# Sums in front of half-size matrix products: twelve of them on GpSimd

## The chip, the cores and the metric

One Trainium2 chip, one of its cores. The metric is the time of one execution of the kernel on the device in microseconds (us). Runs of the kernel before: median 295.94 us, from 295.76 to 295.99. Engines are called as in the profile: PE (TensorE, matrix products), PEld (its weight loads), DVE (VectorE), ACT (ScalarE), POOL (GpSimd), SP (SyncE, here only a queue of DMA issues).

## The reference

Attention with a sliding window of 128 and a linear bias, for 8 batches x 8 heads x 576 positions x 64, and behind it a two-layer network with squared ReLU on the 4608 x 512 result:

```
rel = pos[:, None] - pos[None, :]
scores = scale * q @ k^T - slope_h * |rel|,  masked to 0 <= rel < 128
attn = softmax(scores);  x = (attn @ v) as 4608 x 512
h = x @ w_in              # 512 x 2048
g = relu(h) ** 2
out = g @ w_out           # 2048 x 512, float32
```

## The kernel before

The tokens are cut into 9 groups of 512 (`g` = 0 to 8). For each group the kernel makes the attention, then `h = x @ w_in` ("up"), then the squares, then `out = g @ w_out` ("down"). While the down products of group `g` run, the up products of group `g + 1` run between them, so that PE has always something to do. The last group has only its down products after it.

From group 1 on the down product is made with seven half-size products in place of eight (Strassen-Winograd): the 512 x 2048 block of squares `gs.tile` and `w_out` are each seen as 2 x 2 blocks, and sums of blocks are made in front. The four kinds of sums of the squares are `S1` to `S4` (function `prepare`, lines 1632 to 1662). Each is a bf16 tensor operation over 128 x 1024 elements, and each is cut into two halves `q` = 0, 1 by the feature blocks, so a group has eight of them:

- `S1` = A(21) + A(22), into `sums[:, 0]`; waits for the squares of the group's later 256 tokens (`c12`, `c22`).
- `S2` = S1 - A(11), into `sums[:, 1]`; waits for S1 and the squares of `c11`.
- `S3` = A(11) - A(21), in place in `gs.tile`; waits for S1, which reads the old values, and `c11`.
- `S4` = A(12) - S2, in place; waits for S2 and for product 2, which reads the old values.

Products are named `p<group>.<product>.<token half>`: eight matmuls of 128 x 128 by 128 x 256 (line 1516). Product 5 takes S1, product 6 takes S2, product 7 takes S3, product 3 takes S4; products 1, 2 and 4 take squares as they are. `sums` has one buffer for S1 and one for S2, so S1 of the next group waits until product 5 of this group is done, and S2 until product 6 is.

From group 6 on the up product is made with seven products too (function `up_product`, line 1353 issues its matmuls), for four slices `u` of the features: `f<group>.<u>.<product>`, four matmuls each. Out of PSUM their results go by copies (`s1`, `s2`, `s5`, line 719 on DVE or 721 on ACT) and sums (`c11`, `c22`, `c12`, line 1374 on DVE), each with an ACT ReLU (`relu...`, line 1215) and a square (`sq...`, line 1227 on DVE, 1225 on ACT) behind it. A product of a slice waits for the copy or sum in front of it in the same bank: `f.4` for `c22`, `f.7` for `s2`, `f.6` for `s1`, `f.5` for `c11`, `f.3` for `s5`. The operands of the up products of a group are made by four sums `ut<group>.0` to `.3` (line 1320 on DVE). The down products leave PSUM the same way, by copies `s1_<g>`, `s2_<g>`, `s5_<g>`, `s3_<g>` and sums `c11_<g>` (line 1574), `c22_<g>` (1583), `c12_<g>` (1586). Of the attention, the masks `m<block>` (lines 1022 and 1029), the reciprocals and the normalisation (1121, 1130) are on DVE; its last block is done at about 231 us.

The order on each engine is not written out by hand. Each piece of work is a `Task` with its engine (some with two to choose from), a booked duration, a key, its dependencies and the buffers that it takes and gives back. `Plan.order` lists them once, before the program is written: it goes forward in a booked time and gives each engine the task that can start first, by key among those that can start about as soon. A table `ADJ` shifts keys by name. The program is then written in the order of the booked starts, and each engine works its list strictly in that order. So a changed engine or booked duration of one task changes the order of others, and the choice between DVE and ACT for squares and copies. POOL issues the loads of q, k, v and the weights (lines 812, 815, 867, 872), and does no arithmetic but the `iota` of line 735.

Of the kernel before, what the change touches and what calls it, by code (L numbers as in the profile page):

```python
# [29 lines left out]
S_LEAD = 60  # L30
# [580 lines left out]
def kernel(  # L611
    ctx: ExitStack, tc: tile.TileContext, q, k, v, moe_w_in, moe_w_out, out
):
    nc = tc.nc
# [73 lines left out]
    plan = Plan({**psum_bufs, "rec": 4, "rt": RT, "g": 2, "osb": OSB, "cs": CS, "ut": 2, "s1": 1, "s2": 1, "v0": B, "kqT0": B, "stage": 2, **size})  # L688
# [19 lines left out]
    def dve(n, rate=1):  # L708
        return n / rate / 0.96 + 68.0
# [42 lines left out]
    for part in (1, 0):  # L752
        key = EARLY + 2 if part else -1e5 + 1100
        mkey = -1e5 + 1000 if part else key
        t_dist[part] = plan.add({"DVE": 600.0}, key, lambda part=part: build_dist(part), [t_ident],
                                name=f"dist{part}", later=0.0 if part else 18000.0)
# [13 lines left out]
    for r in range(2):  # L770
        for c in range(4):
            def build_slope(r=r, c=c):
# [5 lines left out]
                else:  # L778
                    nc.scalar.activation(o, dist[:, 1], AF.Copy, bias=0.0, scale=f)
            t_slope[r].append(plan.add({"ACT": act(128), "DVE": dve(128)}, EARLY + 3 + r, build_slope, [t_dist[1]],  # L780
                                       name=f"slope{r}.{c}"))
# [9 lines left out]
    for i in range(size["v"]):  # L791
        t_one["v", i] = plan.add({"DVE": 50.0}, -1e5 + 900 + i, lambda i=i: ones(tiles["v"][i:i + 1]),
                                 name=f"one1.{i}", later=20000.0)
# [99 lines left out]
    def warm_up():  # L893
        bank(s_warm, "wm")
        for _ in range(N_WARM):
            nc.tensor.matmul(s_warm.tile, warm[:, 0:128], warm, start=True, stop=True)
    plan.add({"PE": 430.0 * min(8, N_WARM) + 216.0 * max(0, N_WARM - 8)}, EARLY, warm_up, [t_wz], [s_warm], [s_warm],
             name="warm")
# [728 lines left out]
    def g_sq_at(g):  # L1627
        def sq(half, parts):
            return [x for t in (2 * half, 2 * half + 1) for p in parts for x in sq_of[g, t, p]]
        return sq  # L1630

    def prepare(g, key):

        sq = g_sq_at(g)
        gs = g_slots[g]
        tags = ("ox", "oy") if g % 2 else ("oy", "ox")
        if g >= G_A:
            tags = ("a", "a")
        st = {"slot": {"X": Slot(tags[0]), "Y2": Slot(tags[1]), "Y5": Slot(tags[1]),
                       "S1": Slot("s1"), "S2": Slot("s2")},  # L1640
              "S1": [], "S2": [], "S3": [], "S4": []}
        A, Bk = slice(0, 256), slice(256, 512)

        def add(name, q, out_of, a_of, b_of, op, deps, acq, rel):
            def run():
                nc.vector.tensor_tensor(out_of(), a_of(), b_of(), op=op)  # L1646
            st[name].append(plan.add({"DVE": dve(1024, 2)}, key - S_LEAD + {"S1": 0, "S2": 1, "S3": 2, "S4": 30}[name], run,
                                     deps, acq, rel, name=f"{name}.{g}.{q}"))
        s = st["slot"]
        for q in range(2):  # L1650
            c, d = slice(4 * q, 4 * q + 4), slice(8 + 4 * q, 12 + 4 * q)
            add("S1", q, lambda c=c: sums[:, 0, c], lambda c=c: gs.tile[:, c, Bk], lambda d=d: gs.tile[:, d, Bk], ALU.add,
                sq(1, (q, q + 2)), [] if q else [s["S1"]], [gs])
            add("S2", q, lambda c=c: sums[:, 1, c], lambda c=c: sums[:, 0, c], lambda c=c: gs.tile[:, c, A], ALU.subtract,
                [st["S1"][q]] + sq(0, (q,)), [] if q else [s["S2"]], [gs, s["S1"]])
            add("S3", q, lambda c=c: gs.tile[:, c, Bk], lambda c=c: gs.tile[:, c, A], lambda c=c: gs.tile[:, c, Bk],
                ALU.subtract, [st["S1"][q]] + sq(0, (q,)), [], [gs])
        for q in range(2):
            c, d = slice(4 * q, 4 * q + 4), slice(8 + 4 * q, 12 + 4 * q)
            add("S4", q, lambda d=d: gs.tile[:, d, A], lambda d=d: gs.tile[:, d, A], lambda c=c: sums[:, 1, c],  # L1660
                ALU.subtract, [st["S2"][q]] + sq(0, (q + 2,)), [], [gs, s["S2"]])
        return st
# [44 lines left out]
```

## Time and profile before

| | |
|---|---|
| median of the runs | 295.94 us |
| the profiled execution | 296.17 us, of which span 294.4 us |
| PE busy | 285.1 us |
| DVE busy | 242.1 us |
| ACT busy | 207.7 us |
| POOL busy | 106.6 us, last instruction starts at 194.74 us |
| sums of line 1646 on DVE | 64, 16 of each kind; those of group 6: 218.84 to 237.96 us, of group 7: 246.78 to 265.64 us |

The span is what the profiler saw between the first and the last instruction; the time of the execution has 1.77 us more around it. Busy time counts what an engine is occupied with by its own rows. Rows of one engine overlap a little, since the next instruction starts before the one in front has written all: sums of 0.68 us follow each other every 0.60 us, operations over 128 x 512 bf16 of 0.42 us every 0.33 us. In the timeline equal neighbours are put together in one row (x8 is eight instructions) with the start of the first and the time to the end of the last.

### The profile page before, as it was taken

The numbers are of one execution on the slowest core, as the hardware profiler recorded it, in microseconds if no ns is written. First come the engines' busy times: TensorE is split into PE (matmuls) and PEld (weight loads), VectorE is DVE, ScalarE is ACT, GpSimd is POOL, SyncE is SP. The second block draws the span as 40 slices with busy tenths as digits, with TensorE's granted clock in tenths as the row PEclk, the third lists the DMA queues.
The fourth block names the chain that finished last, engine by engine and source line by source line (L and its number), as shares of the span: only waits on it lengthen the run. The fifth ranks groups of instructions, "written<-read, shape, count | busy, mean of one in ns | idle before, by whom it ended". The sixth has DMA issues, their size and how long they took to land.

```text
span 294.4 us, 8315 instructions
## 1 busy us (share of the span) xinstructions
PE 285.1 (97%) x3279; PEld 224.4 (76%) x3299; DVE 242.1 (82%) x626; ACT 207.7 (71%) x392; POOL 106.6 (36%) x132
## 2 busy tenths in 40 slices
PE   7899999999999999999999999999999999999995
PEld 3588756888888876657666766668889988888884
DVE  5556666879969898869787998999999999799854
ACT  2685454696477766687677898798799778899620
POOL 8944578533817229443855230820000000000000
PEclk9999999999999999999999999999999999999999
DMA  9999999999999999999999999999403211200213
GB/s 124 165 200 207 187 174 181 158 176 143 148 178 179 181 157 157 175 173 147 205 155 156 132 201 136 158 123 174 126 19 92 57 37 38 71 24 14 74 60 121
DMA packets 170792, 39.62 MB, mean 135 GB/s; under 512 B 156800, under 2 KB 170240, under 8 KB 170752
## 3 DMA queue, kind: packets, MB, share of 16 engines
q0 software_dynamic: 115184, 18.10, 91.5%
q1 hardware_dynamic: 54768, 20.33, 40.9%
q10 hardware_dynamic: 800, 0.66, 0.8%
q8 instruction: 26, 0.43, 0.6%
q14 instruction: 14, 0.11, 0.1%
HBM read 36.70 MB, written 9.44 MB: 157 GB/s over the span
## 4 chain that ended last, share of the span: by engine, by line
PE 84%; DMA 5%; POOL 5%; DVE 4%; issue 1%; ACT 0%; POOLq 0%; DVEq 0%
PE o L1516 31%; PE h L1272 14%; PE h L1353 13%; PE h L1254 10%; DMA w_in_sb<-in_moe_w_in_dram 5%; PE s L987 5%; PE pv L1102 5%; PE o L1429 4%; POOL kq L867 2%; POOL vf L872 1%; POOL w_in_sb L812 1%; DVE g L1646 1%; DVE P L1022 1%; DVE x L1130 1%; DVE sums L1646 1%
## 5 line engine op out<-in xcount | busy, mean ns | idle before, releaser
L1215 ACT ACTIVATE rt<-h 128x512 bf16<-128x512 f32 (+1 forms) x109 | 64.7, 595 | 34.2 <-PE h L1254 18.3
L1014 ACT ACTIVATE P<-s 128x512 bf16<-128x512 f32 x120 | 64.0, 602 | 8.2 <-PE s L987 8.0
L1516 PEld LDWEIGHTS <-g 128*128 128x128 bf16 x624 | 59.6, 98 | 9.7 <-DVE g L1646 0.3
L1227 DVE TENSOR_TENSOR g<-rt 128x512 bf16<-128x512 bf16 (+1 forms) x101 | 42.0, 418 | 20.5 <-ACT rt L1215 19.3
L867 POOL DMA_DIRECT2D kq<-in_k_dram x39 | 33.3, 853 | 56.0 <-DMA kqT<-kq 50.7
L1516 PE MATMUL o<-w_out_sb,g 128*128 128x256 bf16 x384 | 47.9, 273 | 0.0
L1254 PE MATMUL h<-xT,w_in_sb 128*128 128x128 bf16 (+1 forms) x512 | 46.2, 246 | 1.0 <-DMA w_in_sb<-in_moe_w_in_dram 0.7
L1272 PE MATMUL h<-xT,w_in_sb 128*128 128x512 bf16 x177 | 45.1, 379 | 0.8 <-issue 0.2
L1254 PEld LDWEIGHTS <-w_in_sb 128*128 128x128 bf16 x512 | 38.8, 98 | 5.1 <-DMA w_in_sb<-in_moe_w_in_dram 1.0
L1022 DVE TENSOR_TENSOR P<-P,masks 128x512 bf16<-128x512 bf16 x96 | 38.6, 417 | 3.1 <-ACT P L1014 1.2
L867 POOL DMA_DIRECT2D kq<-in_q_dram x39 | 33.7, 863 | 8.2 <-DMA w_in_sb<-in_moe_w_in_dram 3.2
L872 POOL DMA_DIRECT2D vt<-in_v_dram x32 | 27.1, 859 | 21.5 <-PE pv L1102 20.7
L1130 DVE TENSOR_TENSOR x<-pv,rec 128x256 bf16<-128x256 f32 (+1 forms) x80 | 32.2, 416 | 0.6
L1516 PE MATMUL o<-wsum,sums 128*128 128x256 bf16 x256 | 31.6, 273 | 0.1
L1516 PE MATMUL o<-wsum,g 128*128 128x256 bf16 x240 | 30.0, 273 | 0.2 <-DVE g L1646 0.2
L1272 PEld LDWEIGHTS <-w_in_sb 128*128 128x128 bf16 x192 | 17.2, 98 | 16.2
L1225 ACT ACTIVATE g<-rt 128x512 bf16<-128x512 bf16 x44 | 27.7, 630 | 1.4
L1516 PEld LDWEIGHTS <-sums 128*128 128x128 bf16 x256 | 24.5, 98 | 3.7 <-DVE sums L1646 0.3
L1102 PEld LDWEIGHTS <-P 128*128 128x128 bf16 x576 | 23.2, 98 | 4.5 <-issue 0.7
L1215 ACT ACTIVATE rt<-vf 128x512 bf16<-128x512 f32 x36 | 22.4, 627 | 5.6 <-DVE vf L1374 5.5
L1374 DVE TENSOR_TENSOR vf<-h,vf 128x512 f32<-128x512 f32 x36 | 24.2, 684 | 1.1 <-PE h L1353 0.8
L721 ACT ACTIVATE osb<-o 128x512 f32<-128x512 f32 x19 | 11.3, 596 | 14.7 <-PE o L1516 12.6
(81 smaller groups left out, 391.6 us busy)
## 6 DMA issues: line engine op xcount, KB each, us to landing
out_dram<-osb SPq DMA_DIRECT2D x53, 128.0 KB, 3.3
kq<-in_k_dram POOLq DMA_DIRECT2D x31, 128.0 KB, 7.4
kq<-in_q_dram POOLq DMA_DIRECT2D x31, 128.0 KB, 7.7
vt<-in_v_dram POOLq DMA_DIRECT2D x24, 128.0 KB, 7.6
w_out_sb<-in_moe_w_out_dram POOLq DMA_DIRECT2D x4, 512.0 KB, 14.5
w_in_sb<-in_moe_w_in_dram POOLq DMA_DIRECT2D x3, 512.0 KB, 10.5
vf<-in_v_dram POOLq DMA_DIRECT2D x8, 128.0 KB, 6.9
out_dram<-osb SPq DMA_DIRECT2D x4, 256.0 KB, 7.0
```

The lines of the kernel that those rows point to most:

```text
L867: nc.gpsimd.dma_start(view(kq[s_kq[m].idx], i), source(src, m, split))
L872: nc.gpsimd.dma_start(tile_of(s_v[m])[0:n, :, 0:D], source(v, m))
L1014: nc.scalar.activation(flat(Pt[sP.idx]), sS[i].tile.rearrange("p (j t) -> p j t", j=2)[:, :, lo:hi], AF.Exp, bias=0.0, scale=scale)
L1022: nc.vector.tensor_tensor(flat(Pt[sP.idx]), flat(Pt[sP.idx]), flat(masks), op=ALU.mult)
L1102: nc.tensor.matmul(sv.tile[0:full, hi * (D + 1):(hi + 1) * (D + 1)], prob, tile_of(s_v[mk])[:, h, 0:D + 1], start=mk == parts[0][1], stop= ...
L1130: nc.vector.tensor_tensor(o, heads(sv)[rows, :, 0:D], sr.tile[rows, :].unsqueeze(2).to_broadcast([n, 4, D]), op=ALU.mult)
L1215: nc.scalar.activation(srt.tile[:, 0:n], i, AF.Relu, bias=0.0, scale=1.0)
L1227: nc.vector.tensor_tensor(o, i, i, op=ALU.mult)
L1254: nc.tensor.matmul(slot.tile[:, f * w:(f + 1) * w], w_in_sb[:, cc, fc * 128:(fc + 1) * 128], xT[:, cc, lo % (XR * 128):lo % (XR * 128) + w ...
L1272: nc.tensor.matmul(slot.tile, w_in_sb[:, cc, fc * 128:(fc + 1) * 128], xT[:, cc, g * 512 % (XR * 128):g * 512 % (XR * 128) + 512], start=c ...
L1353: nc.tensor.matmul(slot.tile[:, j * 256:j * 256 + 256], a, b_, start=fresh and j == 0 and c == 0, stop=c == 1, skip_group_check=True)
L1516: nc.tensor.matmul(slot.tile[:, z * 256:z * 256 + 256], stationary(c), moving(c), start=fresh and z == 0 and c == 0, stop=c == F - 1, skip ...
```

## The change

In groups 6 and 7 the sums S1, S2 and S3, both halves of each, go to POOL as `nc.gpsimd.tensor_tensor` on the same operands, and are booked there with 2300 ns. S4 stays on DVE, and so do all sums of the other groups. Dependencies, buffers and keys are those of before. The plan is made anew with them.

```diff
         def add(name, q, out_of, a_of, b_of, op, deps, acq, rel):
+            if name in ("S1", "S2", "S3") and g in (6, 7):
+                def on_pool():
+                    nc.gpsimd.tensor_tensor(out_of(), a_of(), b_of(), op=op)
+                st[name].append(plan.add({"POOL": 2300.0}, key - S_LEAD + {"S1": 0, "S2": 1, "S3": 2, "S4": 30}[name], on_pool,
+                                         deps, acq, rel, name=f"{name}.{g}.{q}"))
+                return
+
             def run():
                 nc.vector.tensor_tensor(out_of(), a_of(), b_of(), op=op)
             st[name].append(plan.add({"DVE": dve(1024, 2)}, key - S_LEAD + {"S1": 0, "S2": 1, "S3": 2, "S4": 30}[name], run,
```

The order of instructions that comes out of it, before and after, from the first difference of PE on (the rest, from `p7.3.0` to the end, is the same):

```
before  p6.6.0 f7.1.6 p6.5.0 p6.5.1 f7.1.7 f7.0.4 f7.1.5 p6.6.1 f7.2.2 f7.1.3 f7.2.1 p6.7.0 p6.7.1 f7.2.6 f7.1.4 f7.2.5 p6.4.0
after   p6.5.0 p6.5.1 f7.0.4 f7.1.6 f7.1.5 f7.2.2 p6.6.0 f7.1.7 f7.1.3 f7.2.1 p6.6.1 f7.1.4 p6.3.0 f7.2.6 f7.2.5 p6.3.1 f7.2.7
...
before  f8.0.4 f8.1.6 p7.2.1 f8.2.2 f8.1.5 f8.1.7 p7.5.0 f8.2.1 f8.1.3 f8.1.4 p7.6.0 f8.2.6 p7.5.1 f8.2.5 f8.2.7 p7.6.1 f8.2.3
after   f8.0.4 f8.1.6 f8.1.5 p7.2.1 f8.1.7 f8.2.1 f8.1.3 f8.2.2 f8.2.6 f8.1.4 p7.5.0 f8.2.5 p7.6.0 p7.5.1 p7.6.1 f8.2.7 f8.2.3
```

POOL's list ends with S1.6.0, S3.6.0, S2.6.0, S1.6.1, S3.6.1, S2.6.1, S1.7.0, S3.7.0, S2.7.0, S1.7.1, S2.7.1, S3.7.1, behind its last load. On DVE the twelve are gone, and around the second half of group 6 its list is `c12.6.3 s1_6 s1.7.0 c11.7.0 sqc11.7.0 c11_6 S4.6.0 c12.7.0 c22.7.0 c11.7.1 sqc12.7.0 ut8.0 s5_6 ut8.1 s2.7.1 S4.6.1 ut8.2 sqc22.7.0 ut8.3 c22.7.1`. Over the whole program five squares go from ACT to DVE, and one copy of line 719 from DVE to line 721 on ACT.

## The prediction

> **What bounds the kernel now.** I read the busy shares first, then the slices, then the busy time by stage where the twelve sums lie, and last the order of work around one set of three. The page's first two parts:
>
> ```profile
> PE 285.1 (97%) x3279; PEld 224.4 (76%) x3299; DVE 242.1 (82%) x626; ACT 207.7 (71%) x392; POOL 106.6 (36%) x132
> ...
> DVE  5556666879969898869787998999999999799854
> ...
> POOL 8944578533817229443855230820000000000000
> ```
>
> PE is busy for 97% of the span. POOL has nothing to do in the last third (its last instruction, a DMA issue, starts at 194.74 us), so the sums that come to it are in nobody's way on its own queue. The stages of the change (columns: length, busy us and instructions of PE, PEld, DVE, ACT, POOL, granted clock, DMA share, GB/s):
>
> ```profile
> 220.00:240.00 20.00, 20.00 (x222) 18.01 (x215) 19.18 (x42) 16.53 (x29) 0.00 (x0) 1.00 0.23 68
> 240.00:260.00 20.00, 20.00 (x186) 17.94 (x184) 17.58 (x32) 17.01 (x31) 0.00 (x0) 1.00 0.12 41
> 260.00:280.00 20.00, 20.00 (x186) 17.92 (x184) 19.04 (x34) 17.00 (x31) 0.00 (x0) 1.00 0.14 41
> ```
>
> PE never pauses there, at the full clock. In 240 to 260 it does 186 matmuls of 256 columns in 20.00 us, 107.5 ns each, one behind the other without a gap. The chain of waits is PE all the way from 219 to 291 us. So freeing DVE (19.18 + 17.58 + 19.04 = 55.8 of 60 us, idle 4.2) can take nothing off this stage; it can only stop short of adding. From p7.3.0 to the last product PE's order is the same in both kernels, so the end moves only by what PE pauses between 219 and 291.
>
> **What is removed and added.** The rows of the sums, and two others, by tile (min/median/max ns, first and last start):
>
> ```profile
> L1646 DVE TENSOR_TENSOR sums<-g x16: 681/684/693, 68.1 to 278.7; 128x1024 bf16<-128x1024 bf16 x16
> L1646 DVE TENSOR_TENSOR sums<-sums,g x16: 675/683/686, 69.0 to 280.3; 128x1024 bf16<-128x1024 bf16 x16
> L735 POOL IOTA sums<- x1: 344/344/344, 0.8 to 0.8; 128x256 f32 x1
> L777 DVE TENSOR_SCALAR sums<-sums x6: 207/415/668, 1.9 to 2.8; 128x128 bf16<-128x128 f32 x6
> ```
>
> DVE loses twelve instructions of 0.68 us; one follows the next after 0.60 us (263.16, 263.76, 264.36), so 12 x 0.60 = 7.2 us of queue. The plan is made anew with them gone: the order of instructions shows five squares moved from ACT to DVE (g<-rt, spacing 0.33 us: 5 x 0.33 = 1.7) and one PSUM copy moved from DVE to ACT (0.60). DVE's net relief is 7.2 - 1.7 + 0.6 = 6.1 us, worth nothing on a PE that does not pause.
>
> POOL's sum has no row. The only sized POOL arithmetic is the IOTA, one stream of 256 elements in 344 ns; 1024 elements at that pace are 1.38 us, the low end. A sum has three streams (two in, one out); wholly one after another, 3 x 1.38 = 4.13 us, the high end. No row lies nearer to either, so I take the geometric middle, 2.4 us. The Trainium skill (GPSIMD Engine Reference, 3.1 Elementwise) gives 4497 ns for an add of 2048 f32 elements; halved that is an estimate of 2.25 us, by which each set of three below ends 0.5 us sooner and the sum comes out about 0.6 us lower. No run here shows it yet.
>
> Does it fit into the time that the products leave? Take the second half of group 6:
>
> ```profile
> 232.11 0.63 ACT L1225 ACTIVATE g<-rt 128x512 bf16<-128x512 bf16 x1
> ...
> 233.54 0.68 DVE L1646 TENSOR_TENSOR sums<-g 128x1024 bf16<-128x1024 bf16 x1
> 234.26 0.69 DVE L1646 TENSOR_TENSOR g<-g 128x1024 bf16<-128x1024 bf16 x1
> 234.87 0.68 DVE L1574 TENSOR_TENSOR osb<-o,osb 128x512 f32<-128x512 f32 x1
> 235.47 0.68 DVE L1646 TENSOR_TENSOR g<-g,sums 128x1024 bf16<-128x1024 bf16 x1
> 236.07 0.68 DVE L1646 TENSOR_TENSOR sums<-sums,g 128x1024 bf16<-128x1024 bf16 x1
> ...
> 237.02 1.04 PE L1516 MATMUL o<-wsum,sums 128*128 128x256 bf16 x8
> 237.89 0.60 PE L1353 MATMUL h<-ut,kqf 128*128 128x256 bf16 x4
> 238.33 1.91 PE L1516 MATMUL o<-wsum,sums 128*128 128x256 bf16 x16
> ```
>
> The last square that S1.6.1 needs ends on ACT at 232.74, so POOL starts at 232.9. POOL's order is S1, S3, S2. In the new PE order p6.5.0 takes the place at 237.02, then p6.5.1 (237.89), f7.0.4 (238.77), f7.1.6, f7.1.5, f7.2.2, and p6.6.0 at 240.51. p6.5.0 needs S1.6.1: 232.9 + 2.4 + 0.2 = 235.5, early. p6.6.0 needs S2.6.1: 232.9 + 3 x 2.4 + 0.4 (two handovers of 0.2) = 240.5, just in time (0.2 is an allowance of mine; DVE's sum that ends at 233.63 lets ACT start at 233.66). On DVE, S4.6.1 now waits for POOL's S2.6.1, with ut8.2, a square, ut8.3 and c22.7.1 behind it, which PE's next products want; an unheld DVE gets to it at about 240.6, after the 240.3 of S2.6.1, so that wait is free here. So 2.4 us is also the point from which lateness costs: at 2.75 the product waits 1 us, at 4.13 some 5 us. In group 7 POOL can start at 259.5 (last square ends at 259.31 on ACT), its order is S1, S2, S3 and p7.6.0 has been put at about 266.7, which leaves (266.7 - 259.5 - 0.4) / 2 = 3.4 us for each. The first halves of both groups have their three sums done long before anything asks for them: POOL from 218.8 and 246.4, their products not before 237 and 265.
>
> **The term that decides: two engines on one memory.** The twelve POOL sums run for 12 x 2.4 = 28.8 us beside a DVE that is 93% busy. No row shows a POOL instruction that reads SBUF beside DVE work, so I bound it. Low end: DVE is not held at all, 0. High end: DVE is held for the whole of each, 28.8 us, less the relief of 6.1 and the idle 4.2: +18.5 us. What rows say: L777 is one shape, once 207 and once 668 ns, in the microsecond in which POOL issues its first load (1.35 to 2.38 us); DVE was drawn out there by up to 0.46 us with nothing in its own rows that explains it. Against it: the masks of L1022 are 385/419/427 ns over all of 60 to 215 us, beside dozens of POOL's DMA issues; but those issues take no operand out of SBUF, and a sum takes two. I take the first as the nearer row: a DVE instruction whose inputs all lie in SBUF (squares, masks, ut, S4) waits for the POOL sum under way, then POOL's next waits for it; those with an input in PSUM (vf<-h,vf; osb<-o,osb) run on, unless queued behind one that waits, since DVE works in order.
>
> The Trainium skill (SBUF - State Buffer, Who interferes with whom) says that a VectorE instruction with two SBUF inputs and a GpSimd one that reads SBUF lock each other out for a whole instruction. By that rule this term is real and of the size below; were it absent, the sum would be 0 to +1. No run here has shown it yet.
>
> Walked through for the second half of group 6, DVE in its new order: POOL's S1 runs 232.9 to 235.3. The square sqc11.7.0, ready at 234.4, waits to 235.3 (0.33); then c11_6 to 236.23. S3 runs 235.63 to 238.03, S4.6.0 waits for it and ends at 238.63; c12.7.0 ends at 239.23, c22.7.0 at 239.83. PE's f7.0.4, due at 238.77, needs c22.7.0 and starts at 240.03: **1.26 us lost**. S2 runs 238.63 to 241.03; c11.7.1 to 240.43, a square waits to 241.03, then ut8.0, s5_6, ut8.1 and s2.7.1, done at 243.22. PE's f7.1.7, now due at 242.65, needs it: **0.77 us lost**. Together 2.0 us for three sums. With four such sets, 8.0. By means instead: a POOL sum meets about one such DVE instruction (its new order has 23 of them in the 48 us from 219 to 267, one per 2.1 us) and holds it for half its length, 1.2 us, against 0.60 relieved: 12 x 0.6 = 7.2, plus 1.1 for the squares and the copy that changed engine, less the idle 4.2: 4.1. The walk is for a dense set; the sets of group 7 have fewer squares and no masks on DVE. Middle of 4.1 and 8.0: **+6.0 us**. PE, once behind, cannot make it up: it has no idle time left to give.
>
> **The sum.** The profiled execution took 296.17 us (span 294.4, 1.77 around it), 0.23 above the median of the runs, 295.94. 296.17 + 6.0 = 302.2 for such an execution; on the median 295.94 + 6.0 = **301.9**.
>
> **Rivals.** Forecast (0.60): DVE is held, +3 to +10.5, 299 to 306.5.
> *Late sums alone* (0.16): no holding, but a POOL sum takes over 2.4 us; S2.6.1 is late for p6.6.0. At 2.75 us: 232.9 + 8.25 + 0.4 = 241.55 against 240.51, +1.0 (296.9); at 4.13, 245.7 against 240.5 and 268.2 against 266.7, +6.7 (302.6). For it: only 0.0 us of spare at my own middle. Against: one place of four, and three of the four sets have more room.
> *All hidden* (0.17), the one not slower: the engines do not hold each other and a POOL sum takes at most 2.4 us; then every product finds its sum and PE streams on, 295.9. For it: POOL empty, PE's new order leaves the room worked out above, DVE is 6.1 us lighter. Against: L777. It decides at 2.4 us. No gain is in it beyond scatter, as PE has no pause to lose; 0.03 of it for a faster result.
> *Held far more* (0.07): each POOL sum takes over 3 us and meets two DVE instructions, or each is itself drawn out by DVE; 12 x 1.2 more, +11 to +18.5, 307 to 314.
> That the change does not do what it says is excluded: POOL's order has the twelve sums, DVE's has twelve fewer.
>
> **Numbers.** 0.2% (0.6 us) is what a measurement of this kernel can tell from no change. Faster 0.03; within it 0.16 (0.14 of all hidden, 0.02 of late sums); slower 0.81. The range goes from 295.7 (all hidden, with the scatter of 0.2) to 306.5, the forecast's upper end, which leaves out the last rival; slower cases alone fill 296.9 to 306.5.
>
> **What would show it.** Twelve rows of POOL's sums near 2.4 us, start to start. Pauses of PE between 219 and 270, first at f7.0.4 and f7.1.7, ended by DVE vf; idle of DVE before squares, masks and S4 that ends with a POOL sum, or those rows drawn out from 0.42 to up to 2.8 us. If PE waits at p6.6.0 for POOL alone, it is late sums; if it does not pause, all hidden. Wrong altogether would be an end that moves with PE unbroken.

## The result, and the profile after

The changed kernel takes 301.02 us (median of 4 runs, 300.87 to 301.11), the kernel before beside it 295.97; the ratio is 1.0157, 95% interval 1.0118 to 1.0196. It is slower by 5.1 us. In the profiled executions the span grew from 294.4 to 299.1 us.

Busy time of the stages after (columns as before: PE, PEld, DVE, ACT, POOL, granted clock, DMA share, GB/s):

```profile
220.00:240.00 20.00, 18.36 (x194) 16.05 (x193) 18.47 (x32) 13.15 (x23) 10.15 (x6) 1.00 0.23 68
240.00:260.00 20.00, 19.00 (x170) 16.39 (x168) 17.64 (x31) 15.03 (x27) 7.81 (x4) 1.00 0.12 41
260.00:280.00 20.00, 18.77 (x173) 16.66 (x171) 17.85 (x29) 16.88 (x30) 6.34 (x3) 1.00 0.06 17
```

PE, which was busy for 20.00 us of each of these, now pauses for 1.64, 1.00 and 1.23 us, at the full clock. DVE, with fewer instructions than before (32, 31, 29 against 42, 32, 34), is hardly less busy: its instructions have become longer. Rows of POOL's own timeline, from each of its four sets of three sums:

```profile
220.39 2.12 POOL L1647 TENSOR_TENSOR g<-g 128x1024 bf16<-128x1024 bf16 x1
222.47 2.31 POOL L1647 TENSOR_TENSOR sums<-sums,g 128x1024 bf16<-128x1024 bf16 x1
...
236.68 2.19 POOL L1647 TENSOR_TENSOR g<-g 128x1024 bf16<-128x1024 bf16 x1
238.83 2.57 POOL L1647 TENSOR_TENSOR sums<-sums,g 128x1024 bf16<-128x1024 bf16 x1
248.17 2.13 POOL L1647 TENSOR_TENSOR sums<-g 128x1024 bf16<-128x1024 bf16 x1 [6.77 <-ACT g L1225]
...
267.08 2.13 POOL L1647 TENSOR_TENSOR g<-g 128x1024 bf16<-128x1024 bf16 x1
```

and DVE's timeline of the same execution:

```profile
220.44 2.35 DVE L1029 TENSOR_TENSOR P<-P,masks 128x512 bf16<-128x512 bf16 x1 [0.73 <-ACT P L1014]
222.72 0.68 DVE L1374 TENSOR_TENSOR vf<-h,vf 128x512 f32<-128x512 f32 x1
223.32 2.08 DVE L1029 TENSOR_TENSOR P<-P,masks 128x512 bf16<-128x512 bf16 x2
...
237.40 2.01 DVE L1653 TENSOR_TENSOR g<-g,sums 128x1024 bf16<-128x1024 bf16 x1
239.34 1.87 DVE L1374 TENSOR_TENSOR vf<-h,vf 128x512 f32<-128x512 f32 x3
...
248.61 1.97 DVE L1227 TENSOR_TENSOR g<-rt 128x512 bf16<-128x512 bf16 x1
...
267.53 2.23 DVE L1653 TENSOR_TENSOR g<-g,sums 128x1024 bf16<-128x1024 bf16 x1
```

Lay the two side by side. The mask that starts at 220.44, 0.05 us after a POOL sum, should take 0.42 us (the masks of line 1029 before, min/median/max in ns):

```profile
L1029 DVE TENSOR_TENSOR P<-P,masks x16: 385/417/427, 92.2 to 225.8; 128x512 bf16<-128x512 bf16 x16
```

It takes 2.35: the POOL sum ends at 222.51 and the mask at 222.79. S4 (line 1653) starts at 237.40 in the POOL sum that ends at 238.87, and ends at 239.41, 0.54 us behind it. The square at 248.61 ends at 250.58, the POOL sum from 248.17 at 250.30. These distances are the signature of the hold: every drawn-out DVE instruction, eight here and 45 more in the runs with extra sums, copies and quarters below, ends 0.28 to 0.29 us behind the end of a POOL instruction when it is over 128x512, and 0.54 to 0.55 us when it is over 128x1024. All of them are `tensor_tensor` with both inputs in SBUF. The sums `vf<-h,vf`, which read one operand from PSUM, stay at 0.68 us wherever they stand. What that does to PE (its timeline; the rows with a pause in front):

```profile
223.45 0.60 PE L1353 MATMUL h<-ut,w_in_sb 128*128 128x256 bf16 x4 [1.17 <-DVE vf L1374]
225.12 0.35 PE L1102 MATMUL pv<-vt,P 128*128 128x65 bf16 x6 [0.34 <-DVE P L1029]
...
253.02 0.60 PE L1353 MATMUL h<-ut,kqf 128*128 128x256 bf16 x4 [0.55 <-DVE vf L1374]
271.01 0.60 PE L1353 MATMUL h<-ut,kqf 128*128 128x256 bf16 x4 [1.23 <-DVE vf L1374]
```

Each pause is ended by DVE, mostly by a `vf` sum queued behind a drawn-out instruction; none is ended by POOL. With those too short for these rows they add up to 3.87 us in eight pauses. The idle time understates a pause: matmuls of 256 columns follow each other every 0.11 us, but the last one before a pause is shown as busy for 0.27, so that a pause costs about 0.16 us more than its idle time, 5.2 us in all by this estimate. PE starts the stage 0.59 us earlier than in the profile of before (216.63 against 217.22 at product p5.3.0, just in front of it) and ends 4.73 us later (last product at 293.71 against 288.98), so the stage (from p5.3.0 to the last product) cost 5.3 us. By the starts of products common to both orders, 2.25 of them fell to the first set of three sums, 1.7 to the second and third together, 1.4 to the fourth. One execution each of the iotas and of the second halves ran at a granted clock of 0.56 throughout (about 490 us), and one of the quarters took 750.42 us at full clock for a reason that nothing here shows; none of the three is in the medians below.

### The profile page after: what moved, and what is told of

Same layout as the page of the kernel before. It is cut to its first block, busy times and chain, and to the rows that moved or that the text cites. A ratio compares the mean times of both kernels' runs of the same rounds, so it can differ in the third digit from the quotient of the medians.

```text
span 299.1 us, 8345 instructions
## 1 busy us (share of the span) xinstructions
PE 287.6 (96%) x3299; PEld 224.4 (75%) x3299; DVE 244.6 (82%) x618; ACT 205.5 (69%) x388; POOL 132.8 (44%) x144
## 4 chain that ended last, share of the span: by engine, by line
PE 74%; DVE 11%; DMA 6%; POOL 5%; issue 2%; ACT 0%; SPq 0%; DVEq 0%; POOLq 0%
PE o L1516 26%; PE h L1272 14%; PE h L1254 10%; PE h L1353 8%; DMA w_in_sb<-in_moe_w_in_dram 5%; PE s L987 5%; PE pv L1102 5%; PE o L1429 4%; DVE vf L1374 3%; POOL kq L867 2%; DVE g L1653 1%; POOL vf L872 1%; DVE g L1227 1%; POOL w_in_sb L812 1%; DVE vf L719 1%
## 5 line engine op out<-in xcount | busy, mean ns | idle before, releaser
L1227 DVE TENSOR_TENSOR g<-rt 128x512 bf16<-128x512 bf16 (+1 forms) x106 | 46.4, 441 | 21.0 <-ACT rt L1215 19.5
L1272 PE MATMUL h<-xT,w_in_sb 128*128 128x512 bf16 x192 | 46.7, 379 | 0.0
L1647 POOL TENSOR_TENSOR sums<-g 128x1024 bf16<-128x1024 bf16 x4 | 8.6, 2150 | 46.6 <-ACT g L1225 28.8
L1225 ACT ACTIVATE g<-rt 128x512 bf16<-128x512 bf16 x39 | 24.5, 630 | 1.2
```

The costliest lines, as they stand in the source:

```text
L1227: nc.vector.tensor_tensor(o, i, i, op=ALU.mult)
L1272: nc.tensor.matmul(slot.tile, w_in_sb[:, cc, fc * 128:(fc + 1) * 128], xT[:, cc, g * 512 % (XR * 128):g * 512 % (XR * 128) + 512], start=c ...
```

## The experiments

All times are beside the kernel before on the same chip (295.9 to 296.0 us). The theory: DVE instructions whose operands all lie in SBUF are held while POOL runs a sum. The rivals: the sums come late for their products; the new order of the plan costs the time.

**Nothing on POOL.** The edit, in the changed kernel:

```diff
                 def on_pool():
-                    nc.gpsimd.tensor_tensor(out_of(), a_of(), b_of(), op=op)
+                    pass
```

> The changed kernel with its new order on every engine, but the twelve sums on GpSimd are left out (products 5, 6 and 7 of groups 6 and 7 then read stale values), so nothing runs there and nobody waits for it. Theory (DVE instructions with all inputs in SBUF are held for as long as a GpSimd sum runs): with nothing on GpSimd nothing is held, 295.9 us, within 0.6. Rival (the new order itself, with its different choice of DVE and ACT, costs the time): still 299 us or more. Late sums alone: 295.9 too.

Measured: 296.33 us, ratio 1.0011 (0.9994 to 1.0027), and no pause of PE between 216 and 275 us:

```profile
220.00:240.00 20.00, 20.00 (x240) 17.96 (x239) 16.66 (x37) 15.81 (x28) 0.00 (x0) 1.00 0.23 68
240.00:260.00 20.00, 20.00 (x185) 17.92 (x184) 16.28 (x31) 15.86 (x28) 0.00 (x0) 1.00 0.12 41
260.00:280.00 20.00, 20.00 (x185) 17.93 (x184) 17.77 (x32) 16.47 (x29) 0.00 (x0) 1.00 0.13 41
```

From p5.3.0 (217.85) to the last product (289.61) the stage takes 71.76 us, as much as before (217.22 to 288.98). The new order alone is as good as the old one. The 5.1 us come with the sums on POOL.

**Twelve sums too many, reading weights.** The kernel before, in its own order, with this behind the DVE sums (`spare` is a buffer of q and k that is free by then):

```diff
+            if name in ("S1", "S2", "S3") and g in (6, 7):
+                spare = kq[0].rearrange("p (c t) -> p c t", c=4)
+                def extra():
+                    nc.gpsimd.tensor_tensor(spare, w_out_sb[:, 0:4, 0:256], w_out_sb[:, 8:12, 0:256], op=ALU.add)
+                plan.add({"POOL": 2300.0}, key - S_LEAD, extra, deps, name=f"i{name}.{g}.{q}")
```

> The kernel before, order unchanged, all sums on DVE; beside them twelve more sums of the same size on GpSimd, started when the real ones may start, reading only weights and writing a spare buffer, for which nobody waits. Theory (held DVE): DVE is not relieved here and is held as often, so at least the 5.1 us of the change, 301 to 306 us. Rival (late sums: the products wait for GpSimd's results): nothing waits, 295.9 us.

Measured: 320.24 us, ratio 1.0812 (1.0769 to 1.0855), far more than forecast. As the sums read nothing that the kernel makes, nothing tied them to the squares: they started behind the last load, at 197.53, back to back. That makes the clearest picture of the study. POOL's row and DVE's rows beside it:

```profile
197.53 27.47 POOL L1653 TENSOR_TENSOR kq<-w_out_sb 128x1024 bf16<-128x1024 bf16 x12
```

```profile
205.50 0.42 DVE L1130 TENSOR_TENSOR x<-pv,rec 128x256 bf16<-128x256 f32 x1
205.84 0.17 DVE L1121 RECIPROCAL rec<-pv 128x4 f32<-128x4 f32 x1
...
211.14 2.33 DVE L1227 TENSOR_TENSOR g<-rt 128x512 bf16<-128x512 bf16 x1
213.40 2.33 DVE L1298 TENSOR_TENSOR w_in_sb<-w_in_sb 128x512 bf16<-128x512 bf16 x1
215.65 2.60 DVE L1646 TENSOR_TENSOR sums<-g 128x1024 bf16<-128x1024 bf16 x1
218.17 2.33 DVE L1298 TENSOR_TENSOR w_in_sb<-w_in_sb 128x512 bf16<-128x512 bf16 x1
```

Everything with both inputs in SBUF waits out the POOL sum under way and ends about 0.3 us behind it (the large sum 0.55), so that these instructions start 2.26 us apart, 2.52 behind a large one; the normalisation and the reciprocal, which read PSUM, take their 0.42 and 0.17 us in the same stretch. The engines take turns, one instruction each. PE starved: it was busy for 7.62 of the 20 us from 200 to 220, and its granted clock there was 0.77.

**The same at the right time.** The extra sums read squares of the group instead (`gs.tile[:, src, 256:512]` as both operands, `src` the upper feature blocks of the half), so that they start at 215.4, 233.1, 250.1 and 269.4 us, three in a row:

> The kernel before, order unchanged and all sums on DVE; twelve more sums on GpSimd that nobody waits for, now reading squares of groups 6 and 7, so that they start where the moved sums start. Theory (held DVE): three in a row by four, as in the change, but DVE keeps its own sums, which are held too: 302 to 309 us. Rival (late sums): 295.9 us.

Measured: 310.68 us, ratio 1.0503 (1.0438 to 1.0568). Nobody waits for these sums, and they cost 14.8 us. That is against late sums, and 1.7 us above the range of the theory. Two things were not worked into that range: DVE's own large sums were drawn out as well (up to 2.38 us), and PE, waiting for up to 3.2 us at a time, had a granted clock of 0.95 and 0.88 in these two stages:

```profile
240.00:260.00 20.00, 14.95 (x125) 12.50 (x124) 19.34 (x29) 12.27 (x21) 6.07 (x3) 0.95 0.08 27
260.00:280.00 20.00, 17.68 (x141) 14.51 (x139) 16.81 (x24) 13.97 (x24) 6.34 (x3) 0.88 0.12 40
```

**One operand, and none.** With `nc.gpsimd.tensor_copy(spare, gs.tile[:, src, 256:512])` in place of the timed sums:

> As the timed extra sums, but with copies of the same size, which read one operand. If any GpSimd reading of SBUF holds DVE's two-operand instructions: rows of DVE drawn out to the copy's own length, a loss by that length, 296.5 to 302 us. If only GpSimd's second operand does it: 295.9 us and no drawn-out rows.

Measured: 298.76 us, ratio 1.0088 (1.0065 to 1.0111). The rows, by tile and by line:

```profile
L1654 POOL COPY kq<-g x12: 1040/1076/1380, 216.0 to 263.8; 128x1024 bf16<-128x1024 bf16 x12
```

```profile
L1227 DVE TENSOR_TENSOR g<-rt x101: 293/425/1252, 17.1 to 281.9; 128x512 bf16<-128x512 bf16 x99, 128x256 bf16<-128x256 bf16 x2
```

A copy of 1.08 us holds a square for up to 0.83 us: one read operand is enough. With three iotas of 512 f32 in place of each sum, which write and read nothing:

```diff
-                    nc.gpsimd.tensor_tensor(spare, w_out_sb[:, 0:4, 0:256], w_out_sb[:, 8:12, 0:256], op=ALU.add)
+                    for _ in range(3):
+                        nc.gpsimd.iota(kq[0].bitcast(FP32), pattern=[[1, 512]], base=0, channel_multiplier=0,
+                                       allow_small_or_imprecise_dtypes=True)
```

> As the extra sums, but each is replaced by three iotas of 512 f32 elements, some 2.0 us together, which write the spare buffer and read nothing. Theory in its narrow form (GpSimd's reading holds DVE's second input): 295.9 us, within 0.6, squares and masks at their 0.42 us. Wide form (any GpSimd work in SBUF holds DVE): about the time of the extra sums, 300 us or more.

Measured: 296.23 us, ratio 1.0002 (0.9982 to 1.0023). The iotas once more:

> The thirty-six extra iotas once more for a look at an undisturbed profile: they start after the last load, at about 195 us, back to back for 20 us, where the extra sums on weights ran too. Narrow form (GpSimd's reading holds DVE): squares, masks and sums of DVE at 0.42 and 0.68 us throughout, 295.9 us. Wide form: rows of 0.6 to 1.0 us there.

Measured: 295.72 us in the one run. The rows of POOL, and of DVE's squares:

```profile
L1654 POOL IOTA kq<- x36: 557/558/677, 192.8 to 214.8; 128x512 f32 x36
```

```profile
L1227 DVE TENSOR_TENSOR g<-rt x101: 291/425/430, 17.2 to 278.9; 128x512 bf16<-128x512 bf16 x99, 128x256 bf16<-128x256 bf16 x2
```

POOL is busy for 17.8 of the 20 us from 195 to 215, where DVE was stopped by the extra sums on weights, and no square goes over 0.43 us. That each iota is short (0.56 us) does not explain it: in the next experiment sums of 0.66 us draw masks out to 0.88. The narrow form holds: it is POOL's reading of SBUF.

**Shorter sums on POOL.** In the changed kernel each sum is cut along its four feature blocks, into two instructions and into four (here four):

```diff
-                    nc.gpsimd.tensor_tensor(out_of(), a_of(), b_of(), op=op)
+                    for i in range(4):
+                        w = slice(i, i + 1)
+                        nc.gpsimd.tensor_tensor(out_of()[:, w], a_of()[:, w], b_of()[:, w], op=op)
```

> The changed kernel, each of the twelve sums cut into two GpSimd instructions of 512 elements. Theory (a hold lasts to the end of the GpSimd instruction under way, and PE loses what goes beyond the slack of its order): holds up to 1.1 us, between those of whole sums (5.1 us lost) and of quarters (1.0 us lost), 297.5 to 299.5 us. Rival (late sums): no better than whole sums, 301 us.

> The changed kernel, each of the twelve sums cut into four GpSimd instructions of 256 elements (some 0.6 us each, 2.4 us together). Theory (a hold lasts to the end of the GpSimd instruction under way): holds are a quarter as long, at most 0.6 us, so a quarter to a half of the 5.1 us is left, 297.2 to 298.6 us. Rival (late sums): GpSimd ends its sums no sooner, 301 us or a little more.

Measured: halves 298.39 us, ratio 1.0080 (1.0058 to 1.0103); quarters 296.96 us, ratio 1.0026 (1.0009 to 1.0043). The masks of line 1029 in halves and in quarters:

```profile
L1029 DVE TENSOR_TENSOR P<-P,masks x16: 386/418/1340, 91.6 to 226.2; 128x512 bf16<-128x512 bf16 x16
```

```profile
L1029 DVE TENSOR_TENSOR P<-P,masks x16: 386/418/884, 92.0 to 227.3; 128x512 bf16<-128x512 bf16 x16
```

The longest mask falls from 2.35 to 1.34 and 0.88 us. POOL's work does not get shorter (four quarters took 2.5 to 3.2 us together, a whole sum 2.1 to 2.6), so late sums would not have lost less by that. A piece can start before the whole sum's squares are there, though (the first two quarters at 215.92 and 216.55, the first whole sum at 218.10), so against late sums this experiment says less than the extra sums, for which nobody waits. Adding up by how much single DVE instructions that start between 212 and 276 us exceed the normal length of their form gives 8.6 us in eight instructions for whole sums, 6.0 in 11 for halves, 4.6 in 15 for quarters, while the loss goes 5.1, 2.4, 1.0 us. So the loss is not proportional to the held time. It fits that short holds vanish in the slack of PE's order and long ones come through. The forecast for quarters, 297.2 at the least, was a little too high; that slack was not in it.

**Half of the sums.** `q == 0` or `q == 1` added to the condition of the change; the plan is made anew for each.

> Only the first halves (q = 0) of S1, S2, S3 of groups 6 and 7 go to GpSimd, six sums; the plan is made anew. Their products ask for them over 10 us after they are done. Theory (held DVE): each set of three costs where it meets DVE's squares and masks, as the sets at 218 and 248 us do in the changed kernel (2.2 and some 0.7 us of PE's time): 297.5 to 299.5 us. Rival (late sums): nothing is late, 295.9 us.

> Only the second halves (q = 1) go to GpSimd, six sums; the plan is made anew. Theory (held DVE): the sets at 234 and 263 us cost some 1.0 and 1.4 us of PE's time, 297.3 to 299.3 us. Rival (late sums): here alone products follow soon, so all of the 5.1 us must show, 301 us.

Measured: first halves 299.66 us, ratio 1.0123 (1.0098 to 1.0148); second halves 298.60 us, ratio 1.0081 (1.0061 to 1.0102). The first halves, which nobody is waiting for, cost time all the same: late sums fall here too. But 299.66 is above the forecast, and the pauses do not lie as it had them. PE pauses at the first set (1.17, 0.33 and 0.14 us from 223.98 on) and nowhere at the second, whose sums run from 248.58 to 255.07; and it pauses near 281 us, 25 us after POOL's last sum. Hence, the same kernel with its six sums left out as in the first experiment:

> The kernel with only the first halves on GpSimd, in its own order, with those six sums left out (products of groups 6 and 7 read stale values). Its profile showed 1.6 us of PE's time gone at 220 to 226 us and pauses of some 1.0 us at 279.7 to 281.5, long after GpSimd's last sum. If the holds cost all: 295.9 us. If the second pauses come from the new order itself: 296.9 us, with the same pauses near 280.

Measured: 297.16 us, ratio 1.0024 (1.0000 to 1.0047), with the pauses at 279.0 and 279.8 us (POOL idle). So 1.2 of the 3.7 us are an order that came out a little worse, at the edge of what the runs can tell from nothing, and 2.5 us are the sums'. The stage says the same: from p5.3.0 to the last product it takes 72.69 us without the sums and 75.20 with them, against 71.76 before. The second halves once more:

> The kernel with only the second halves on GpSimd once more, for an undisturbed profile: PE's pauses lie behind the sums at 233 and 262 us, each behind a drawn-out square or S4 on DVE; none at 220 to 226 us, where nothing runs on GpSimd.

Measured: 298.86 us in the one run, PE unbroken up to 238 us, then pauses of 0.13, 0.16, 0.21 and 1.28 us ended by DVE `vf`, the last behind the S4 that starts at 265.17 and takes 2.28 us beside a POOL sum from 264.78 to 266.91.

## Why the prediction was right

- **What bounds the kernel.** Right. PE had no pause to lose, DVE's relief of 6.1 us bought nothing (without the sums, 296.3 us), and the change went into new pauses of PE.
- **POOL's sum.** Taken as 2.4 us between 1.38 and 4.13; it is 2.12 to 2.57, most of them 2.13 to 2.19. The estimate from the Trainium skill (GPSIMD Engine Reference, 3.1 Elementwise), 2.25 us, was the nearer one; the trace agrees within 6%.
- **Whether the sums fit.** Right: S2.6.1 ended at 241.40 and p6.6.0 ran at 242.41, S1.6.1 at 236.60 and p6.5.0 at 238.68. No pause of PE is ended by POOL.
- **The deciding term.** Right in kind and sign, and in the stage, but only in part in the place: the first pauses were forecast at f7.0.4 and f7.1.7, where 0.56 us were lost, while the longest came at the first set (before 223.45) and at the fourth (before 271.01). The Trainium skill (SBUF - State Buffer, Who interferes with whom) says that a VectorE instruction with two SBUF inputs and a GpSimd one that reads SBUF lock each other out for the whole instruction; this case's traces agree, with rows of 2.33 us for 0.42 beside sums of 2.13 to 2.3, and 0.42 beside iotas.
- **Its size.** Forecast +6.0 (301.9 us), measured +5.1 (301.02). The +6.0 was the middle of two workings, and both were off in parts; that the middle came so near is partly luck. The walk for the second set gave 1.26 us lost at f7.0.4 and 0.77 at f7.1.7; it was 0.23 and 0.33. At f7.0.4 the difference can be counted: the two POOL sums in front were 0.27 and 0.21 us shorter than 2.4, the second began 0.08 us behind the first and not 0.33, and PE's product 0.04 us behind the sum that it waits for and not 0.2. The first set, not walked, cost 2.25 us, where masks of the last attention block met POOL twice. The working by means erred twice, in opposite directions: it had twelve holds of 1.2 us (14.4), where the trace has 8.6 in eight instructions, and it credited the relief and DVE's idle time against them, which by the measured 8.6 would leave no loss at all (8.6 - 6.1 - 4.2 is below zero). Idle time of DVE elsewhere does not pay for an instruction that is late here.
- **Rivals.** All hidden fell with the 5.1 us that the change costs, late sums with the extra sums and the first halves, and because no pause of PE is ended by POOL. Held far more did not occur in the change, but is what the extra sums show when DVE keeps its own large sums.
- **Not settled.** The order of the second halves was not run without its sums. In the extra sums on weights the first held mask starts at 196.79, 0.74 us before the first POOL sum's row, and yet ends 0.29 us behind that sum; no run shows what held it until then. No DVE instruction that reads one input, and that from SBUF, stood beside a POOL sum, so whether such a one is held stays open. A kernel whose DVE has no all-SBUF instruction beside POOL's sums was not tried. None of the versions beats the kernel before.

## What to carry to other kernels

Moving elementwise work from DVE to an idle POOL does not add a second engine when both read SBUF: here each DVE `tensor_tensor` with both inputs there waited out the POOL instruction under way, and everything queued behind it waited too. If POOL must help, cut its instructions until one hold is shorter than the slack of the consumer (here 0.7 us instead of 2.1 took the loss from 5.1 to 1.0 us), or, which was not tried, put them where DVE reads from PSUM. And before relieving an engine, look whether the one that sets the end ever waits for it.

## What the runs showed of the hardware that was not expected

- The two engines take turns: with twelve POOL sums back to back, DVE got eleven all-SBUF instructions in, one for each sum except the one beside which it had only PSUM readers to run, 2.26 us apart at 0.42 us of work. POOL hardly slowed: its sums started 2.27 us apart on average, against 2.08 to 2.29 us within the sets of the change.
- A POOL copy, reading one operand, holds DVE as a sum does, for its own shorter time (1.08 us); thirty-six iotas, writing only, hold nothing.
- Where PE was starved for microseconds at a time its granted clock was lower as well: 0.77 and 0.72 from 200 to 240 us beside the extra sums on weights, 1.00 again from 240 us on. In the change, with pauses of at most 1.23 us, it stayed at 1.00.
- ScalarE did not notice: of its 38 instructions beside POOL's sums in the change, none took over 0.05 us longer than the longest of its form before.
